# One Strassen level in the first product of the second MoE, on 768-token tiles, with its weights kept in DRAM

## The chip, the cores and the metric

The kernel runs on one core of one Trainium2 chip. TensorE (PE in the rows) multiplies matrices, VectorE (DVE), ScalarE (ACT) and GpSimd (POOL) work element by element, SyncE (SP) issues most DMAs. The metric is the device time of one execution in microseconds, as a median of several executions; lower is better.

## What is computed

Attention with a local and a downsampled part gives 2304 tokens of width 512; two MoE-like blocks follow. The last one, on which the change works, is `moe2`:

```python
def _moe_ref(x, w1, w2, w3, w_out):
    h = np.maximum(np.maximum(x @ w1, x @ w2), x @ w3)
    return h @ w_out                      # d_ff = 768

def _moe2_ref(x, w_in, w_out):            # x: 2304 x 512, d_ff = 2048
    h = np.maximum(x @ w_in, 0.0)
    return (h * h @ w_out)
```

The weights arrive as float64 words (128x512 of them are 512 KB) and are decoded to fp32 on the chip.

## The kernel before

Every fp32 product is made of three float32r matmuls (`mm3`): each operand is split into a rounded part `hi` and a rest `lo`, and hi·hi, hi·lo and lo·hi are summed in PSUM. `hi` is a ScalarE or VectorE copy with rounding, `lo` a subtraction on VectorE or GpSimd.

The tokens of a batch element (576) stand in two halves of 256 and 320. The program goes through the four batch elements; while TensorE does the first MoE (`moe1`) of element b, the other engines prepare the attention of element b+1. A table of tokens (`CFG`) gives the order: `G01` is one gate unit (three 4x3-matmul products of half 0, feature block 1), `Y02` one output unit of `moe1`, whose result goes to DRAM (`yscr`). `CFG["last"]` is the stretch for the last element, with `e` for one decoded weight tile of `moe2`. TensorE's instructions stand in the order in which they are written; a scheduler places those of the other engines, except that VectorE's order was also written out by hand from this stretch on.

`moe2` works on six tiles t of 384 tokens (`T2`). For each of 16 blocks f of 128 features, `in_unit` makes x·w_in (12 matmuls of 384 columns, tile `i`) into one of four PSUM banks, ScalarE and VectorE make relu, square and the split (`r`, `g`, `gh`, `gl`), and `out_unit`, called one block later, adds the block's share to three output banks (9 matmuls of 512 columns, tile `po`). All 32 weight tiles stay in SBUF after the first tile; they are decoded (`split_late`) during `last` and t = 0: VectorE rebiases (L98), shifts (L135), joins (L107, L110) and rounds (L143), GpSimd subtracts (L144). Raw words land in three buffers (`stg`).

Of the kernel before, what the change touches and what calls it, by code (L numbers as in the profile page):

```python
# [8 lines left out]
F32 = mybir.dt.float32  # L9
F32R = mybir.dt.float32r  # L10
# [8 lines left out]
P = 128  # L19
# [17 lines left out]
    "t0": "1111110201211120",  # L37
# [16 lines left out]
        "e e e G13 e e G02 e G11 e G12 G00 G10 e e G03 e G01 G14 G15 e Y13 G04 e Y10 e G05 e e e "  # L54
        "Y12 Y03 Y02 Y00 Y11 Y01 e e"
# [5 lines left out]
def local_global_attention__then__moe_kernel(  # L61
# [18 lines left out]
    T2 = 384  # L80
# [7 lines left out]
        for b in range(B)  # L88
    ]
# [40 lines left out]
    def split_late(items):  # L130
        parts = []
        work = [raw_words(src, name) for src, name, *_ in items]
        for low, high in work:
            rebias(high)
            nc.vector.tensor_scalar(  # L135
                out=low, in0=low, scalar1=29, scalar2=None, op0=ALU.logical_shift_right
            )
            join(low, high, low)
        for (src, name, pool, tag, bufs), (low, high) in zip(items, work):
            w = low.bitcast(F32)  # L140
            hi = pool.tile([P, 512], F32R, tag=tag, name=f"hi_{name}", bufs=bufs)
            lo = pool.tile([P, 512], F32R, tag=tag, name=f"lo_{name}", bufs=bufs)
            nc.vector.tensor_copy(hi, w)  # L143
            nc.gpsimd.tensor_tensor(out=lo, in0=w, in1=hi.bitcast(F32), op=ALU.subtract)  # L144
            parts.append((hi, lo))
        return parts

    def mm3(ps, whi, wlo, xhi, xlo, first, last):
        nc.tensor.matmul(ps, whi, xhi, start=first, stop=False)  # L149
        nc.tensor.matmul(ps, whi, xlo, start=False, stop=False)  # L150
        nc.tensor.matmul(ps, wlo, xhi, start=False, stop=last)  # L151
# [322 lines left out]

    w2_t = {}
    w2_todo = [(kind, f) for f in range(NF2) for kind in ("i", "o")]

    def load_w2(n=1):
        keys = w2_todo[:n]
        at = 2 * NF2 - len(w2_todo)  # L480
        del w2_todo[:n]
        items = []
        for i, (kind, f) in enumerate(keys):
            where = (w2, "w2", 12) if at + i < 6 else (wpool, "w", 36) if at + i < 24 else (gp, "w2", 16)
            items.append(((wi2 if kind == "i" else wo2)[f], f"{kind}2{f}", *where))
        if items:
            w2_t.update(zip(keys, split_late(items)))

    yt = {}
    NT2 = NT // T2  # L490

    def load_y(t, gq, pool):
        hi = pool.tile([P, NP, T2], F32R, tag="yh", name=f"yh{t}", bufs=1)
        lo = pool.tile([P, NP, T2], F32R, tag="yl", name=f"yl{t}", bufs=1)
        for k0 in range(0, NP, 2):
            raw = gq.tile([P, 2, T2], F32, tag="yr", name=f"yr{t}{k0}", bufs=1)
            t0, done = t * T2, 0
# [14 lines left out]
        yt[t] = (hi, lo)

    with tc.manual_schedule(engines={ENG.PE}):
# [26 lines left out]
        dve_order = ExitStack()  # L541
        dve_order.enter_context(tc.manual_schedule(engines={ENG.DVE}))
        at.close()
        w2 = ctx.enter_context(tc.tile_pool(name="w2", bufs=12, reuse_waits="tile"))
        gq = ctx.enter_context(tc.tile_pool(name="gq", bufs=1, reuse_waits="tile"))
        ps_o = ctx.enter_context(tc.tile_pool(name="ps_o", bufs=1, space=PSUM, reuse_waits="tile"))
        load_y(0, gq, gq)
        run(B - 1, CFG["last"])
        p1.close()

        gp = ctx.enter_context(tc.tile_pool(name="gp", bufs=2, reuse_waits="tile", side="right"))
        ps_i = ctx.enter_context(tc.tile_pool(name="ps_i", bufs=4, space=PSUM, reuse_waits="tile", side="right"))
        g_t = {}
        po = {}

        def in_unit(t, f):
            ps = ps_i.tile([P, 512], F32, tag="i", name=f"i{t}_{f}")
            hi, lo = w2_t["i", f]
            yhi, ylo = yt[t]
            for kc in range(NP):  # L560
                ks = slice(kc * P, (kc + 1) * P)
                mm3(ps[:, 0:T2], hi[:, ks], lo[:, ks], yhi[:, kc, :], ylo[:, kc, :], kc == 0, kc == NP - 1)
            r = gp.tile([P, T2], F32, tag="r", name=f"r{t}_{f}")
            g = gp.tile([P, T2], F32, tag="g", name=f"g2{t}_{f}")
# [11 lines left out]
        def out_unit(t, f):
            if f == 0:
                po[t] = [
                    ps_o.tile([P, DM], F32, tag=f"o{i}", name=f"po{t}_{i}") for i in range(T2 // P)
                ]  # L580
            ghi, glo = g_t.pop((t, f))
            whi, wlo = w2_t["o", f]
            for i in range(T2 // P):
                ts = slice(i * P, (i + 1) * P)
                mm3(po[t][i], ghi[:, ts], glo[:, ts], whi, wlo, f == 0, f == NF2 - 1)
                if f == NF2 - 1:
                    o = gp.tile([P, DM], F32, tag="ob", name=f"ob{t}_{i}", bufs=3)
                    if i % 2:
                        nc.vector.tensor_copy(o, po[t][i])
                    else:  # L590
                        nc.scalar.activation(out=o, in_=po[t][i], func=AF.Copy)
                    r0 = t * T2 + i * P
                    nc.sync.dma_start(out=out[r0 : r0 + P, :], in_=o)
# [62 lines left out]
```

## Time and profile before

| | |
|---|---|
| median of three executions | 874.84 us (874.76 to 878.05) |
| the profiled execution | 878.28 us, its span 876.4 us |
| TensorE busy | 833.2 us, 95% of the span |
| VectorE, ScalarE, GpSimd busy | 477.7, 278.6, 214.0 us |
| mean granted TensorE clock | 0.985 |
| `moe2`, from its first matmul to the last output copy | 462.9 to 872.0 us |

The span runs from the first to the last instruction of the profiled execution. Busy shares are an average over very different stretches, so the stretches below are read one by one.

### The profile page before, as it was taken

Reading aid. Unit: us, or ns where it says so; the run is one execution under the profiler, and the core shown is the slowest. Engines: PE = TensorE matmul, PEld = TensorE weight load, DVE = VectorE, ACT = ScalarE, POOL = GpSimd, SP = SyncE. Lnnn points to the kernel's source line nnn. Section 1 sums busy time; section 2 is a strip of 40 time slices with the busy share of each in tenths; the row PEclk is TensorE's granted clock in tenths of the full one; section 3 lists DMA queues with packets and bytes.
Section 4 is the critical chain, followed back from the end, with each engine's and each line's share of the span. In section 5 each row is a group of like instructions: output and inputs, shape, how many; then the busy total and the mean of one; then the engine's idle time right before and its main releaser. Section 6 shows DMA issues by size and latency. Waiting matters only on the chain.

```text
span 876.4 us, 15330 instructions
## 1 busy us (share of the span) xinstructions
PE 833.2 (95%) x6160; PEld 770.2 (88%) x6160; DVE 477.7 (55%) x938; ACT 278.6 (32%) x669; POOL 214.0 (24%) x260
## 2 busy tenths in 40 slices
PE   5588989999999999998998999999999999999997
PEld 4377989999999999998997889989999899989996
DVE  7998996525663375676789984223223223223222
ACT  3455533413342233421113333223223223223222
POOL 4745484400533032142135333001001001000000
PEclk9997999999999999998999999999999999999999
DMA  7735443400232011143245332002002001000001
GB/s 242 222 109 174 132 148 93 141 16 29 80 98 75 1 56 59 32 142 106 73 139 167 123 120 73 1 0 73 1 1 73 1 1 54 1 1 37 1 1 37
DMA packets 39831, 64.15 MB, mean 73 GB/s; under 512 B 4464, under 2 KB 23760, under 8 KB 39760
## 3 DMA queue, kind: packets, MB, share of 16 engines
q1 hardware_dynamic: 35152, 58.46, 21.5%
q10 hardware_dynamic: 4608, 4.72, 1.6%
q8 instruction: 48, 0.79, 0.4%
q14 instruction: 23, 0.19, 0.1%
HBM read 53.73 MB, written 9.44 MB: 72 GB/s over the span
## 4 chain that ended last, share of the span: by engine, by line
PE 83%; DVE 10%; DMA 3%; issue 1%; ACT 1%; POOL 0%; SPq 0%; DVEq 0%; ACTq 0%; POOLq 0%
PE g L149 8%; PE g L150 8%; PE g L151 7%; PE po L151 7%; PE po L150 7%; PE po L149 7%; PE i L149 7%; PE i L151 7%; PE i L150 7%; PE yp L149 3%; PE yp L151 3%; PE yp L150 3%; DMA q<-in_qT 1%; DMA raw_g<-in_wg 1%; DVE lo_g L126 1%
## 5 line engine op out<-in xcount | busy, mean ns | idle before, releaser
L149 PE MATMUL g<-xhi,hi_g 128*128 128x256 f32 (+1 forms) x576 | 177.0, 307 | 6.6 <-DVE c L407 6.6
L150 PE MATMUL g<-xlo,hi_g 128*128 128x256 f32 (+1 forms) x576 | 173.9, 302 | 1.5 <-DVE xlo L368 1.5
L151 PE MATMUL g<-xhi,lo_g 128*128 128x256 f32 (+1 forms) x576 | 174.0, 302 | 0.0
L567 DVE TENSOR_TENSOR g<-r 128x384 f32<-128x384 f32 x80 | 46.1, 577 | 193.3 <-ACT r L565 193.3
L149 PE MATMUL i<-yh,hi_i 128*128 128x384 f32 x384 | 129.6, 338 | 0.5 <-ACT ys L433 0.5
L151 PE MATMUL i<-yh,lo_i 128*128 128x384 f32 x384 | 129.4, 337 | 0.0
L150 PE MATMUL i<-yl,hi_i 128*128 128x384 f32 x384 | 129.3, 337 | 0.0
L149 PEld LDWEIGHTS g<-xhi,hi_g 128*128 128x128 f32 x576 | 112.4, 195 | 9.0 <-DVE c L407 7.6
L565 ACT ACTIVATE r<-i 128x384 f32<-128x384 f32 x96 | 47.2, 491 | 227.1 <-PE i L151 227.1
L151 PE MATMUL po<-hi_o,gl 128*128 128x512 f32 x288 | 114.3, 397 | 2.0 <-DVE gl L573 2.0
L149 PE MATMUL po<-hi_o,gh 128*128 128x512 f32 x288 | 113.8, 395 | 1.6 <-ACT gh L572 1.6
L150 PEld LDWEIGHTS g<-xlo,hi_g 128*128 128x128 f32 x576 | 113.0, 196 | 1.7 <-DVE xlo L368 1.7
L150 PE MATMUL po<-lo_o,gh 128*128 128x512 f32 x288 | 114.1, 396 | 0.0
L151 PEld LDWEIGHTS g<-xhi,lo_g 128*128 128x128 f32 x576 | 112.1, 195 | 0.0
L573 DVE TENSOR_TENSOR gl<-g,gh 128x384 fp32r<-128x384 f32 x96 | 54.5, 568 | 54.1 <-ACT gh L572 54.1
L407 DVE TENSOR_TENSOR c<-g,c 128x256 f32<-128x256 f32 (+1 forms) x96 | 43.6, 455 | 69.2 <-PE g L151 67.4
L149 PEld LDWEIGHTS i<-yh,hi_i 128*128 128x128 f32 x384 | 72.1, 188 | 4.9 <-ACT ys L433 0.7
L150 PEld LDWEIGHTS i<-yl,hi_i 128*128 128x128 f32 x384 | 72.1, 188 | 4.1
L509 POOL TENSOR_TENSOR yl<-yr,yh 128x384 fp32r<-128x384 f32 x24 | 26.8, 1135 | 196.7 <-ACT yh L508 196.7
L151 PEld LDWEIGHTS i<-yh,lo_i 128*128 128x128 f32 x384 | 72.1, 188 | 0.0
L151 PEld LDWEIGHTS po<-hi_o,gl 128*128 128x128 f32 x288 | 54.2, 188 | 17.7 <-DVE gl L573 4.6
L572 ACT ACTIVATE gh<-g 128x384 fp32r<-128x384 f32 x96 | 50.3, 524 | 49.0 <-DVE g L567 46.5
(1057 smaller groups left out, 1380.0 us busy)
## 6 DMA issues: line engine op xcount, KB each, us to landing
raw_o<-in_wo SPq DMA_DIRECT2D x22, 512.0 KB
raw_g<-in_wg SPq DMA_DIRECT2D x18, 512.0 KB
raw_i<-in_wi SPq DMA_DIRECT2D x16, 512.0 KB
k<-in_kT SPq DMA_DIRECT2D x16, 291.0 KB
q<-in_qT SPq DMA_DIRECT2D x16, 288.0 KB
v<-in_vP SPq DMA_DIRECT2D x32, 144.0 KB
out_y<-ob SPq DMA_DIRECT2D x18, 256.0 KB
vw<-in_vP SPq DMA_DIRECT2D x16, 175.0 KB
```

What stands on the lines that cost most here:

```text
L126: eng.tensor_tensor(out=lo, in0=w, in1=hi.bitcast(F32), op=ALU.subtract)
L149: nc.tensor.matmul(ps, whi, xhi, start=first, stop=False)
L150: nc.tensor.matmul(ps, whi, xlo, start=False, stop=False)
L151: nc.tensor.matmul(ps, wlo, xhi, start=False, stop=last)
L407: nc.vector.tensor_tensor(out=c, in0=ps[:, 0:N], in1=c, op=ALU.max)
L509: nc.gpsimd.tensor_tensor(out=lo[:, kc], in0=raw[:, kc - k0], in1=hi[:, kc].bitcast(F32), op=ALU.subtract)
L565: nc.scalar.activation(out=r, in_=ps[:, 0:T2], func=AF.Relu)
L567: nc.vector.tensor_tensor(out=g, in0=r, in1=r, op=ALU.mult)
L572: nc.scalar.activation(out=ghi, in_=g, func=AF.Copy)
L573: nc.vector.tensor_tensor(out=glo, in0=g, in1=ghi.bitcast(F32), op=ALU.subtract)
```

## The change

`moe2` now takes three tiles of 768 tokens, and eight quads q of 256 features each. One quad's product x·w_in is a 2x2 block product (384 tokens x 256 inputs by 256 inputs x 128 features, twice each way), and is made with seven block products P1 to P7 in place of eight, by Winograd's form of Strassen's method. A block product is 6 matmuls of 384 columns, into two PSUM banks in turn (`x`, `y`); P2 is added onto P1's bank and P3 onto P5's after VectorE or ScalarE have read them. Sums of token blocks (`S1` to `S4`, `y_sums`) and of weight blocks (`sums` in `decode_quad`) are made by VectorE, and so are the sums of products: `u2`, `u3` and three of the four output blocks `c`, each read from PSUM with a second input from SBUF. The output matmuls of a quad (12 groups of 3) are spread between the products of the next quad.

A quad's six pairs of weight tiles (`i0` to `i3`, `o0`, `o1`, hi and lo) live in four sets of buffers for eight quads. So each decoded quad is also stored to a DRAM scratch (`wscr`, 12 stores), and tiles 1 and 2 read four of the eight quads back (`load_quad`). Quads 0 to 2 are decoded during `last`, quads 3 to 7 during tile 0. `last` has lost its `e` tokens, and its units stand in the order of the features. VectorE's order is left to the scheduler.

```diff
-    T2 = 384
+    T2 = 768
+    TH = T2 // 2
+    NT2 = NT // T2
+    NQ = NF2 // 2
+    PRODUCTS = (
+        ("P1", "A11", "i0", 0), ("P6", "S2", "i1", 256), ("P2", "A12", "i0", 256), ("P7", "S3", "i2", 0),
+        ("P5", "S1", "i1", 0), ("P4", "A22", "i2", 256), ("P3", "S4", "i3", 0),
+    )
...
+    def split_cut(q, c, w, c0=0):
+        n = w.shape[-1]
+        hi, lo = w2_t[q][c + "h"][:, c0 : c0 + n], w2_t[q][c + "l"][:, c0 : c0 + n]
+        nc.scalar.activation(out=hi, in_=w, func=AF.Copy)
+        nc.gpsimd.tensor_tensor(out=lo, in0=w, in1=hi.bitcast(F32), op=ALU.subtract)
...
+        def sums():
...
+            nc.vector.tensor_tensor(out=t1, in0=b12, in1=b11, op=ALU.subtract)
+            nc.vector.tensor_tensor(out=t3, in0=b22, in1=b12, op=ALU.subtract)
+            nc.vector.tensor_tensor(out=t2, in0=b22, in1=t1, op=ALU.subtract)
+            nc.vector.tensor_tensor(out=t4, in0=t2, in1=b21, op=ALU.subtract)
...
+        return [
+            lambda: begin("f0", wi2[f]),
+            lambda: begin("f1", wi2[f + 1]),
+            both,
+            other,
+            sums,
+            lambda: (split_cut(q, "i1", tb["f0"]), begin("o0", wo2[f]), stores("i0", "i3")),
+            lambda: (split_cut(q, "i2", tb["f1"]), begin("o1", wo2[f + 1]), stores("i1", "i2")),
+            lambda: last("o0", "o0"),
+            lambda: (last("o1", "o1"), stores("o0", "o1")),
+        ]
...
+                if p == "P1":
+                    got["p1"] = f("p1", "p", 1)
+                    A.activation(out=got["p1"], in_=d, func=AF.Copy)
+                elif p == "P6":
+                    got["u2"] = f("u2", "u2", 1)
+                    V.tensor_tensor(out=got["u2"], in0=d, in1=got["p1"], op=ALU.add)
...
+                elif p == "P7":
+                    got["u3"] = f("u3", "u3", 1)
+                    V.tensor_tensor(out=got["u3"], in0=d, in1=got["u2"], op=ALU.add)
+                elif p == "P5":
+                    e = f("c", "c22", 3)
+                    V.tensor_tensor(out=e, in0=d, in1=got["u3"], op=ALU.add)
+                    square("22", e)
...
+                for call in outs[len(outs) * j // 7 : len(outs) * (j + 1) // 7]:
+                    call()
...
+        spread(0, 0, [lambda a=a: y_split(0, a, nc.vector) for a in ("S1", "A22", "S4")], 0)
+        spread(0, 0, decode_quad(3))
+        for q in range(4, NQ):
+            spread(0, q - 3, decode_quad(q), 2)
+        turns = [list(range(NQ)), [4, 5, 6, 7, 0, 1, 2, 3], list(range(NQ))]
```

Where the instructions went is seen in the built programs. VectorE before, one block of t = 0 (`raw_o210` is a raw weight tile, `gl0_4` the rest of the squared features of block 4 that `out_unit` multiplies):

```order
L98 TENSOR_SCALAR raw_o210_6107<-raw_o210_6107 128x512
L135 TENSOR_SCALAR raw_o210_6107<-raw_o210_6107 128x512
L107 SCALAR_TENSOR_TENSOR raw_o210_6107<-raw_o210_6107 128x512
L110 SCALAR_TENSOR_TENSOR raw_o210_6107<-raw_o210_6107 128x512
L143 CAST hi_o210_6113<-raw_o210_6107 128x512
L573 TENSOR_TENSOR gl0_4_6144<-g20_4_6140,gh0_4_6143 128x384
```

VectorE now, half of quad 3 of tile 0 (`u303` is u3 of tile 0, quad 3; L108 rebiases, L117 and L120 join, of raw words of quads 5 and 6):

```order
L737 TENSOR_TENSOR u303_6660<-P7_03_6653,u203_6608 128x384
L671 TENSOR_TENSOR gl0311_6636<-c1103_6632,gh0311_6635 128x384
L740 TENSOR_TENSOR c2203_6684<-P5_03_6677,u303_6660 128x384
L714 SCALAR_TENSOR_TENSOR c2203_6684<-c2203_6684 128x384
L108 TENSOR_SCALAR raw_o1_5_6618<-raw_o1_5_6618 128x512
L671 TENSOR_TENSOR gl0322_6688<-c2203_6684,gh0322_6687 128x384
L744 TENSOR_TENSOR c2103_6720<-u303_6660,P4_03_6713 128x384
L117 SCALAR_TENSOR_TENSOR raw_o1_5_6618<-raw_o1_5_6618 128x512
L714 SCALAR_TENSOR_TENSOR c2103_6720<-c2103_6720 128x384
L120 SCALAR_TENSOR_TENSOR raw_o1_5_6618<-raw_o1_5_6618 128x512
L748 TENSOR_TENSOR c1203_6743<-P5_03_6677,u203_6608 128x384
L671 TENSOR_TENSOR gl0321_6724<-c2103_6720,gh0321_6723 128x384
```

Decoding and the reads of PSUM for which TensorE waits now alternate on one in-order engine. SyncE's queue before, in the same stretch, held raw loads alone:

```order
L93 DMA raw_i211_6147<-in_wi2 128x512
L93 DMA raw_o211_6187<-in_wo2 128x512
L93 DMA raw_i212_6257<-in_wi2 128x512
L93 DMA raw_o212_6267<-in_wo2 128x512
L93 DMA raw_i213_6353<-in_wi2 128x512
```

SyncE's queue now, as quad 4 is stored and quad 5 begun (`s4i1l` is the scratch copy of the lo part of cut i1 of quad 4):

```order
L501 DMA s4i1h_121<-w4i1h_6337 128x512
L501 DMA s4i1l_122<-w4i1l_6338 128x512
L103 DMA raw_o1_4_6437<-in_wo2 128x512
L501 DMA s4i2h_123<-w4i2h_6339 128x512
L501 DMA s4i2l_124<-w4i2l_6340 128x512
L103 DMA raw_f0_5_6468<-in_wi2 128x512
L501 DMA s4o0h_127<-w4o0h_6343 128x512
L501 DMA s4o0l_128<-w4o0l_6344 128x512
L103 DMA raw_f1_5_6492<-in_wi2 128x512
```

Each raw load now stands behind stores that wait for ScalarE and GpSimd.

## Rows read from the trace of the kernel before

**Rows 1.** The page's busy times: us (share of span) x instructions.

```profile
PE 833.2 (95%) x6160; PEld 770.2 (88%) x6160; DVE 477.7 (55%) x938; ACT 278.6 (32%) x669; POOL 214.0 (24%) x260
```

**Rows 2.** Stretches: length, then PE, PEld, DVE, ACT, POOL busy, clock, DMA share, GB/s.

```profile
0.00:378.90 378.90, 347.89 (x3570) 327.44 (x3571) 253.76 (x566) 142.81 (x393) 141.30 (x205) 0.98 0.33 100
378.90:462.90 84.00, 79.99 (x577) 79.32 (x575) 65.27 (x114) 15.49 (x37) 26.41 (x20) 0.96 0.38 120
462.90:535.00 72.10, 68.46 (x338) 60.08 (x339) 63.92 (x94) 27.06 (x54) 31.38 (x22) 1.00 0.38 115
602.00:872.00 270.00, 269.91 (x1346) 242.93 (x1344) 75.91 (x133) 73.85 (x148) 10.60 (x11) 1.00 0.06 20
```

**Rows 3.** PE in order of time, steady `moe2`: start, duration, instruction.

```profile
600.56 0.34 PE L149 MATMUL i<-yh,hi_i 128*128 128x384 f32 x1
...
602.67 0.40 PE L149 MATMUL po<-hi_o,gh 128*128 128x512 f32 x1
...
604.76 0.34 PE L149 MATMUL i<-yh,hi_i 128*128 128x384 f32 x1
```

**Rows 4.** PE's waits from 380 us on: total us, times, longest.

```profile
PE g L149 <- DVE c L407: 3.5, 2, 2.8
PE po L151 <- DVE gl L573: 2.0, 4, 1.1
PE po L149 <- ACT gh L572: 1.6, 1, 1.6
```

**Rows 5.** PE in order of time around the longest of these waits.

```profile
397.54 0.63 PE L149 MATMUL g<-xhi,hi_g 128*128 128x320 f32 x1 [2.77 <-DVE c L407]
397.97 0.47 PE L150 MATMUL g<-xlo,hi_g 128*128 128x320 f32 x1
...
403.55 0.31 PE L150 MATMUL g<-xlo,hi_g 128*128 128x320 f32 x1
403.70 0.31 PE L151 MATMUL g<-xhi,lo_g 128*128 128x320 f32 x1
```

**Rows 6.** VectorE's groups in 462.9 to 535 us: busy us, mean ns, idle before.

```profile
L573 DVE TENSOR_TENSOR gl<-g,gh 128x384 fp32r<-128x384 f32 x16 | 9.6, 599 | 6.4 <-ACT gh L572 6.4
L98 DVE TENSOR_SCALAR raw_o<-raw_o 128x512 f32<-128x512 f32 x8 | 9.0, 1123 | 0.0
L107 DVE SCALAR_TENSOR_TENSOR raw_o<-raw_o 128x512 uint32<-128x512 uint32 x8 | 6.3, 782 | 0.3
```

**Rows 7.** The split `gl` in 535 to 800 us, the same columns.

```profile
L573 DVE TENSOR_TENSOR gl<-g,gh 128x384 fp32r<-128x384 f32 x63 | 35.5, 563 | 37.6 <-ACT gh L572 37.6
```

**Rows 8.** VectorE reading PSUM in 378.9 to 462.9 us, two widths.

```profile
L407 DVE TENSOR_TENSOR c<-g,c 128x320 f32<-128x320 f32 x12 | 5.9, 489 | 4.9 <-PE g L151 4.5
L407 DVE TENSOR_TENSOR c<-g,c 128x256 f32<-128x256 f32 x12 | 5.1, 423 | 4.0 <-PE g L151 3.4
```

**Rows 9.** GpSimd's subtraction in 395 to 560 us.

```profile
L144 POOL TENSOR_TENSOR lo_o<-raw_o,hi_o 128x512 fp32r<-128x512 f32 x14 | 20.5, 1465 | 47.6 <-DVE hi_o L143 39.5 <-PE g L151 5.5 <-issue 2.7
```

**Rows 10.** VectorE in order of time around 501 us.

```profile
500.34 0.70 DVE L110 SCALAR_TENSOR_TENSOR raw_i<-raw_i 128x512 uint32<-128x512 uint32 x1
...
501.42 0.42 DVE L98 TENSOR_SCALAR raw_o<-raw_o 128x512 f32<-128x512 f32 x1
501.75 1.54 DVE L135 TENSOR_SCALAR raw_o<-raw_o 128x512 uint32<-128x512 uint32 x1
```

**Rows 11.** GpSimd at the same time.

```profile
501.58 1.43 POOL L144 TENSOR_TENSOR lo_i<-raw_i,hi_i 128x512 fp32r<-128x512 f32 x1 [3.63 <-DVE hi_i L143]
```

**Rows 12.** SyncE's DMA queue: packets, MB, share of 16 engines' span.

```profile
q1 hardware_dynamic: 35152, 58.46, 21.5%
```

**Rows 13.** Issue of half a token tile (0.79 MB in two DMAs) on SyncE.

```profile
385.61 0.89 SPq L503 DMA_DIRECT2D yr<-y  x2
```

**Rows 14.** ScalarE: the first use of that half, and the last output copy.

```profile
389.40 0.94 ACT L508 ACTIVATE yh<-yr 128x384 fp32r<-128x384 f32 x2 [0.58 <-DMA yr<-y]
...
871.95 0.60 ACT L591 ACTIVATE ob<-po 128x512 f32<-128x512 f32 x1 [0.79 <-PE po L151]
```

More of the change, by code (lines that the diff above doesn't have):

```diff
@@ L88, in local_global_attention__then__moe_kernel @@
         for b in range(B)
+    ]
+    wscr = [
+        {
+            c + e: yd.tile([P, 256 if c == "i3" else 512], F32, name=f"s{q}{c}{e}", tag=f"s{q}{c}{e}")
+            for c in CUT
+            for e in "hl"
+        }
+        for q in range(NQ)
     ]
@@ L128, in split_mid, with mm3 @@
         return parts
[L130 to L151, printed above, removed]
+    def mm3(ps, whi, wlo, xhi, xlo, first, last, more=False):
+        nc.tensor.matmul(ps, whi, xhi, start=first, stop=False, skip_group_check=more)
+        nc.tensor.matmul(ps, whi, xlo, start=False, stop=False, skip_group_check=more)
+        nc.tensor.matmul(ps, wlo, xhi, start=False, stop=last, skip_group_check=more)
     p1 = ExitStack()
@@ new lines, in load_quad, with part, y_sums, load @@
+    def load_quad(q):
+        def part(cuts, new=False):
+            if new:
+                quad_tiles(q)
+            for c in cuts:
+                n = 256 if c == "i3" else 512
+                for e in "hl":
+                    nc.sync.dma_start(out=w2_t[q][c + e][:, 0:n].bitcast(F32), in_=wscr[q][c + e])
+        return [lambda: part(CUT[:4], True), lambda: part(CUT[4:])]
+    def y_sums(t):
+        blocks = y2_t[t] = {}
+        def load():
+            raw = yq.tile([P, NP, T2], F32, tag="yr", name=f"yr{t}")
@@ L576, in out_unit @@
[L576 to L593, printed above, removed]
@@ L595, in local_global_attention__then__moe_kernel @@
[L595 to L608 removed]
+        yq = ctx.enter_context(tc.tile_pool(name="yq", bufs=1, reuse_waits="tile"))
@@ new lines, in local_global_attention__then__moe_kernel @@
+        ps_i = ctx.enter_context(tc.tile_pool(name="ps_i", bufs=1, space=PSUM, reuse_waits="tile"))
+        back = y_sums(0)
+        back += [lambda a=a: y_split(0, a, nc.vector) for a in EARLY]
+        for q in range(3):
+            back += decode_quad(q)
+        units = CFG["last"].split()
+        done = 0
+        for i, token in enumerate(units):
+            run(B - 1, token)
+            while done < len(back) * (i + 1) // len(units):
+                back[done]()
+                done += 1
@@ new lines, in local_global_attention__then__moe_kernel, with product @@
+        p1.close()
+        gp = ctx.enter_context(tc.tile_pool(name="gp", bufs=1, reuse_waits="tile", side="right"))
+        ps_o = ctx.enter_context(tc.tile_pool(name="ps_o", bufs=1, space=PSUM, reuse_waits="tile"))
+        po = {}
+        def product(t, q, ps, a, c, c0, first):
+            whi, wlo = w2_t[q][c + "h"], w2_t[q][c + "l"]
+            yhi, ylo = y2_t[t][a + "x"]
+            for kc in range(2):
+                ks = slice(c0 + kc * P, c0 + (kc + 1) * P)
+                mm3(ps[:, 0:TH], whi[:, ks], wlo[:, ks], yhi[:, kc, :], ylo[:, kc, :], first and kc == 0, kc == 1, not first)
@@ new lines, in local_global_attention__then__moe_kernel @@
+        for t, k in ((1, 0), (1, 1), (1, 2), (1, 3), (2, 0), (2, 1), (2, 2), (2, 3)):
+            one, two = load_quad(turns[t][k + 4])
+            spread(t, k + 1, [one], 1)
+            spread(t, k + 2, [two], 1)
+        for t in range(NT2 - 1):
+            spread(t, 5, y_sums(t + 1), 0, 2)
+            for j, (_, a, _, _) in enumerate(PRODUCTS):
+                spread(t, NQ - 1, [lambda t=t, a=a, j=j: y_split(t + 1, a, nc.gpsimd if j % 2 else nc.vector)], j)
+        outs = []
+        y_split(0, "S3", nc.vector)
@@ L611 @@
+        for t in range(NT2):
+            for k, q in enumerate(turns[t]):
+                outs = quad(t, k, q, outs, between[t, k])
+        for call in outs:
+            call()
 def kernel(**inputs):
```

218 lines of the change are left out of this document (146 added, 72 removed).

## The prediction

> **What bounds the kernel now.** I read the page's busy times first: TensorE is busy 95% of the span, VectorE 55%, GpSimd 24% [rows 1]. Such a share says nothing of a single stretch, so the windows by stage come next [rows 2]. From 602 us on, TensorE is busy 269.91 of 270 us while VectorE has 76 us of work: there only fewer or shorter matmuls save time. From 378.9 to 535 us the picture is another. In the last stretch of the first MoE and in the first tile of `moe2`, VectorE is busy 65.27 of 84.00 and 63.92 of 72.10 us, and GpSimd adds 26 and 31 us. That is where the weights are decoded, and the change puts more work for both engines there.
>
> TensorE's own timeline gives the price of a matmul: 12 of 384 columns take 602.67 − 600.56 = 2.11 us, 0.176 each, and 9 of 512 columns 2.09 us, 0.232 each [rows 3]. Its waits from 380 us on are few: 3.5 us on VectorE's `c` at the gates, 3.6 us on the splits `gl` and `gh` at the start of `moe2` [rows 4]. After the longest, 2.77 us, the next 22 matmuls stand (403.55 − 397.54) / 22 = 0.273 us apart, against 0.15 from 403.55 on: the level of 1.2 GHz, where 22 x 0.123 = 2.7 us are lost [rows 5].
>
> **What is removed.** Before, `moe2` has 96 blocks of 12 matmuls, 1152; now 24 quads of 7 x 6, 1008. 144 matmuls at 0.176: −25.3 us. The output matmuls stay 864. A quad takes TensorE 42 x 0.176 + 36 x 0.232 = 15.74 us. The two waits at the gates with the slow clock behind one of them come from VectorE's handwritten order, in which decoding stood before `c`; the scheduler's order has the `c` first: −3.5 − 2.7 = −6.2, with 1.0 given back because seven passes over 128x768 tokens (0.95 us each, from the slope of 423 to 489 ns for 64 more columns [rows 8]) now stand among the first gates. Four PSUM banks hide most of these. The 3.6 us of waits at the start of `moe2` go with the code in which they stood.
>
> **The first quad** has no output groups to put between its products, which follow each other at 1.06 us, 7.4 in all. Before TensorE can take a bank for quad 1, VectorE must do four token splits of 768 (3.8 us), four reads of PSUM at 0.56 (the same slope, at 384 columns), and the three passes between them (1.8), and the first split can start some 2 us late, behind ScalarE's last copy of the first MoE: 9.8 us. +2.4.
>
> **Quads 1 to 5 of the first tile** are the heart of it. From u2 of quad 1 to u2 of quad 6, VectorE's order holds 17 rebias, 34 joins, 16 weight sums of 256 columns, 4 token sums of 768 and 65 passes of 384 over products. At the durations of the first tile before, 1.1 us for a rebias, 0.78 for a join, 0.6 for a pass in SBUF [rows 6], 0.56 for the 25 that read PSUM, 0.42 for a sum (as the 256-column row [rows 8]), that is 18.7 + 26.5 + 6.7 + 3.8 + 24 + 14 = 93.7 us. TensorE needs 5 x 15.74 = 78.7. VectorE is in order, and u2, u3 and `c` are what TensorE waits for before it may write a bank again; a bank is free some 3.5 us late before that hurts, once, not per quad. So +15. The lower bound is the same list undisturbed: 0.42 for a rebias, 0.70 for a join [rows 10], 0.56 for a pass [rows 7]: 78 us, +0. The disturbance is seen in one place: a tensor_scalar of 0.42 us took 1.54 when it came 0.17 us after a GpSimd subtraction of 1.43 had begun [rows 10, 11]. The upper bound is that the two engines take turns throughout, below under the rivals. I take the durations as they stood in the first tile before, since GpSimd's share was the same 43% there.
>
> The Trainium skill (SBUF — State Buffer, Who interferes with whom) says that GpSimd and VectorE share one pair of ports as an exclusive lock, and that VectorE operations with two SBUF inputs take part in it, not only the fast single-input ones. The 1.54 us agrees for the latter; for the two-input `gl` the rows show 599 ns beside a busy GpSimd against 563 without, and no pure case. By that rule the term would be +17 to +31 in place of +15.
>
> **Raw words.** A decoded quad loads 4 x 524 KB and stores 2.88 MB, 4.98 MB. The SyncE queue moved 58.46 MB in 21.5% of 876.4 us, 310 GB/s when all is busy [rows 12]; so 16.1 us a quad, under the 18.7 that VectorE needs: hidden, with little to spare. Half a token tile took 3.8 us from issue to use [rows 13, 14], so a raw tile some 3. Between the last weight sum and the next quad's first rebias stand about 13 VectorE instructions, 8 us, which must cover ScalarE's and GpSimd's split, the issue and the landing, 6.5 to 7.5 us. I take +1, between 0 and the rival below.
>
> **Small terms.** The tokens of tile 2 are asked for when GpSimd has split the last block of tile 1, and take about 6.3 us to land (3.8 and 0.79 MB more at 310 GB/s), while VectorE waits for them in quad 0 of tile 1 with u3 behind: +1, between 0 and 3. One wait long enough to lower the clock: +1, between 0 and 5 (2.7 each). The last output copy finds two buffers in place of three and waits for the DMA of the copy two before it: +0.9, between 0 and 1.9 (from the 4.45 us between 871.95 and the span's end [rows 14], less the 2.8 us between the two). The reloads of tiles 1 and 2 have over 40 us before their first use, VectorE needs 13 x 0.56 = 7.3 of 15.74 us there, and GpSimd nothing but token splits: no cost.
>
> **Sum.** −25.3 − 6.2 + 1.0 − 3.6 + 2.4 + 15 + 1 + 1 + 1 + 0.9 = −12.8 us on a span of 876.4 us: 863.6. The profiled execution took 878.28 us, 1.9 outside its span, and is 3.4 above the median; taken off the median of 874.84, the sum gives 862.0.
>
> **The rivals.**
> - Decoding stays covered. For it: the undisturbed list needs 78 us, no more than TensorE. Against it: the rows of the first tile, where VectorE was never undisturbed. Without the 15 and the clock: 846.
> - VectorE and GpSimd take turns. Its place is the same five quads. All but the 25 reads of PSUM shut GpSimd out: 78 − 14 = 64 us undisturbed, and GpSimd has the like of 22 subtractions at 1.465 us [rows 9], 32: 96 us if the PSUM reads all run beside GpSimd, 110 if none does, +17 to +31. The first tile before speaks for it: 63.92 + 31.38 is 95 us in 72.1, and the excess of 23 is about what the VectorE rows are longer than undisturbed. This is the skill's rule above. At +24: 871.
> - Raw words come late, the side on which the change loses. Place: each rebias at VectorE's head waits for a DMA that stands behind stores on SyncE; u2, u3 and `c` wait behind it. Each 256 KB store ahead of a raw tile adds 0.85 us. Four ahead of each quad's first load cost 3.4 us a quad; if the 17 waits add up to 13 us the gain is gone, and from 17 us (1 us each) the kernel is slower by over 0.5%. With 5 us a quad and more at the other loads: 880 to 890.
> - The saving is not had in the steady quads: a bank is not read in time in every quad. For it: two banks in place of four. Against it: each read has 3 us, VectorE and ScalarE are half idle. At 1 us a quad: 885.
>
> **How the numbers follow.** Forecast (853 to 870) 0.42, covered 0.20, taking turns beyond it 0.14, late raw words 0.15, steady quads late 0.06, slow clock over much of the first tile 0.03 (870). The range runs from the covered case to the point where late words have taken all: 846 to 878. Half a per cent, 4.4 us, is about what a measurement of this kernel can tell from no change. Faster by more: the first two, half of the third and a little of the others, 0.70. Within: 0.15. Slower: 0.15.
>
> **What would show it.** PE matmuls on the products 1008 at 0.176 and quads of 15.7 us in tiles 1 and 2; the first tile 140 to 146 us long in place of 126, its waits on VectorE's u2, u3 and `c` reads and not on ScalarE; VectorE over 95% busy there with rebias near 1.1 us; the gates' wait of 2.77 gone. VectorE idle behind raw DMAs in quads 1 to 5 would show the third rival, joins at 1 us and more the second. I am wrong if the first tile takes under 132 or over 155 us, or a quad of tile 1 over 16.5.

## The result, and the profile after

The changed kernel takes 866.02 us in the median of four executions (864.85 to 866.37), the kernel before 874.80: a ratio of 0.989, with a 95% interval of 0.9864 to 0.9916. The forecast was 862.0, so that 8.8 of the 12.8 us were gained. The two profiled executions stand further apart than the medians: that of the kernel before took 878.28 us, 3.5 above its median, that of the changed kernel 864.85, 1.2 below. Its span is 863.1 us, against a forecast of 863.6.

Between these two executions the total agrees to half a microsecond, in part by this luck; in which stage the 4.6 us lie that they have over the medians, no trace shows. The stages do not agree, and they are what the experiments had to explain. The page's busy times of the changed kernel, to be read beside [rows 1]:

```profile
PE 809.9 (94%) x6016; PEld 741.7 (86%) x6016; DVE 561.0 (65%) x1072; ACT 298.5 (35%) x679; POOL 220.7 (26%) x258
```

TensorE has 144 instructions fewer, VectorE 134 more and 83 us more to do. The stretches, with the columns of [rows 2], are cut here at the last attention product of the last batch element (372.25, where the last stretch of the first MoE begins), the first product of `moe2` (462.52), u2 of quads 1 and 6 of the first tile (477.41, 570.49), u2 of the second tile's first quad (600.48) and the end of the matmuls:

```profile
0.00:372.25 372.25, 336.95 (x3438) 315.95 (x3439) 254.38 (x565) 141.34 (x384) 139.32 (x204) 0.94 0.32 100
372.25:462.52 90.27, 89.32 (x714) 88.14 (x710) 60.46 (x99) 36.85 (x77) 23.39 (x18) 1.00 0.61 203
462.52:477.41 14.89, 12.52 (x65) 10.78 (x64) 12.81 (x17) 9.83 (x18) 7.84 (x5) 1.00 0.54 185
477.41:570.49 93.08, 82.79 (x395) 70.18 (x394) 85.67 (x138) 39.38 (x72) 38.34 (x25) 1.00 0.69 238
570.49:600.48 29.99, 29.99 (x151) 26.93 (x150) 18.80 (x32) 11.65 (x19) 5.88 (x3) 1.00 0.09 30
600.48:859.00 258.52, 258.05 (x1269) 229.72 (x1267) 128.89 (x225) 58.87 (x110) 5.92 (x3) 1.00 0.33 110
```

The same cuts in the trace of the kernel before lie at 367.22 (that attention product) and 462.88 (the first product). The two profiled executions then differ so:

| stage | before | after | forecast | measured |
|---|---|---|---|---|
| up to the last attention product | 367.22 | 372.25 | 0 | +5.0 |
| last stretch of the first MoE | 95.66 | 90.27 | −5.2 | −5.4 |
| first product to last output copy | 409.07 | 396.87 | −8.5 | −12.2 |
| last output copy to the end | 4.45 | 3.71 | +0.9 | −0.7 |
| span | 876.4 | 863.1 | −12.8 | −13.3 |

The last row of that count, with [rows 14] for the kernel before, is ScalarE's last output copy:

```profile
859.39 0.60 ACT L687 ACTIVATE ob<-po 128x512 f32<-128x512 f32 x1 [2.14 <-PE po L143]
```

A loss of 5.0 us that the forecast did not have lies before any instruction of `moe2` on TensorE, and it is hidden in the total by 3.7 us in `moe2` and 1.6 at the end that came out better. It is no accident of one execution: in the eight traces of this document that decode quad 0 so early, this attention product stands at 370.8 to 373.3 us, in the kernel before at 367.2 and in its variant below (before_lovec) at 366.7.

The stretch that the forecast called the heart, u2 of quad 1 to u2 of quad 6, takes 93.08 us where the forecast had 93.7 and TensorE needs 78.7. TensorE's waits from 462.52 to 600.48 us, in total, how often, and the longest:

```profile
PE P L141 <- DVE u L737: 4.6, 3, 1.9
PE P L141 <- DVE c L748: 3.5, 4, 1.2
PE P L141 <- DVE c L744: 1.3, 1, 1.3
PE P L141 <- DVE c L740: 1.2, 2, 1.0
PE P L141 <- ACT c L732: 1.0, 2, 0.7
PE P L141 <- ACT p L726: 0.7, 1, 0.7
PE P L141 <- DVE u L729: 0.2, 1, 0.2
```

10.8 of 12.5 us are waits for VectorE's reads of a bank (u2, u3, `c`), none is over 2 us, and the granted clock stays at 1.00. VectorE's largest groups in that stretch, with the columns of [rows 6]:

```profile
L671 DVE TENSOR_TENSOR gl<-c,gh 128x384 fp32r<-128x384 f32 x21 | 16.8, 800 | 2.4 <-ACT gh L670 2.2
L714 DVE SCALAR_TENSOR_TENSOR c<-c 128x384 f32<-128x384 f32 x15 | 10.4, 695 | 0.1
L117 DVE SCALAR_TENSOR_TENSOR raw_o<-raw_o 128x512 uint32<-128x512 uint32 x9 | 9.0, 996 | 0.2
L733 DVE TENSOR_TENSOR c<-c 128x384 f32<-128x384 f32 x5 | 4.4, 885 | 0.0
L108 DVE TENSOR_SCALAR raw_o<-raw_o 128x512 f32<-128x512 f32 x9 | 3.8, 422 | 2.6 <-DMA raw_o<-in_wo 2.6
L729 DVE TENSOR_TENSOR u<-P,p 128x384 f32<-128x384 f32 x6 | 3.3, 549 | 0.0
```

The forecast wanted VectorE over 95% busy and the rebias at 1.1 us. It is 92% busy (85.67 of 93.08), the rebias of `raw_o` takes 0.42 and that of `raw_f` 0.52, and the long ones are the passes with two inputs in SBUF: `gl` 0.80, the first join 1.00. The reads of PSUM (u2) stay at 0.55. GpSimd in order of time, and VectorE beside it, show why:

```profile
507.23 1.41 POOL L496 TENSOR_TENSOR w4o1l<-raw_o,w4o1h 128x512 fp32r<-128x512 f32 x1 [2.65 <-ACT w4o1h L495]
510.02 1.60 POOL L496 TENSOR_TENSOR w5i0l<-raw_f,w5i0h 128x512 fp32r<-128x512 f32 x1 [1.38 <-ACT w5i0h L495]
```

VectorE at the same time:

```profile
507.38 0.54 DVE L744 TENSOR_TENSOR c<-u,P 128x384 f32<-128x384 f32 x1
507.85 1.33 DVE L120 SCALAR_TENSOR_TENSOR raw_f<-raw_f 128x512 uint32<-128x512 uint32 x1
509.11 0.54 DVE L671 TENSOR_TENSOR gl<-c,gh 128x384 fp32r<-128x384 f32 x1
509.57 0.55 DVE L714 SCALAR_TENSOR_TENSOR c<-c 128x384 f32<-128x384 f32 x1
510.04 0.41 DVE L108 TENSOR_SCALAR raw_f<-raw_f 128x512 f32<-128x512 f32 x1
510.38 0.54 DVE L748 TENSOR_TENSOR c<-P,u 128x384 f32<-128x384 f32 x1
510.85 1.32 DVE L117 SCALAR_TENSOR_TENSOR raw_f<-raw_f 128x512 uint32<-128x512 uint32 x1
```

Each of the two GpSimd subtractions has several VectorE passes beside it. The one that reads PSUM takes its 0.54, the rebias at 510.04 its 0.41. The join after them, 0.68 when alone, ends some 0.5 us after the subtraction does (509.18 against 508.64, 512.17 against 511.62), as if it had begun its work only then. This is the forecast's rival "VectorE and GpSimd take turns", and it became the first theory to test.

To put a size on it: the sum of all VectorE durations in the stretch less each form's count times its shortest duration there is the excess. For `gl` it is 21 x (0.80 − 0.55) = 5.3 us; over all forms it is 19.1 us, beside 38.3 us of GpSimd.

The 5.0 us before the last stretch start at one row of TensorE. It is the last of five transpositions for the second batch element:

```profile
139.66 0.30 PE L298 MATMUL t10B<-const,sm10B 128*70 128x128 f32 x1 [3.81 <-DVE x3210F L352]
```

In the trace before, all five stood together, without a wait:

```profile
136.13 0.74 PE L306 MATMUL t10B<-const,sm10B 128*70 128x128 f32 x5
```

VectorE does x3210F at 139.18 us, behind three rebias, six joins and four sums of quad 0's raw words that it began at 127.63. Before, one raw tile's decoding stood there. The scheduler had pulled the decoding of a weight that is needed at 462 us forward to 127. Behind the wait the granted clock is 0.50, the level of 1.2 GHz, for a while (142 to 144 us), and from the first of the five to the product behind them (o10B) it takes 15.25 us (135.21 to 150.46) in place of 9.52 (136.13 to 145.65): 5.7 more. The granted clock was also lower than before in the first part of this execution (0.50 in place of 1.00 from 20 to 40 us), but at the first transposition TensorE was still 0.9 us ahead of the trace before, so the 5.0 us are not from there.

### The profile page after: what moved, and what is told of

It reads as the page before. It is cut to its first block, busy times and chain, and to the rows that moved or that the text cites. A ratio compares the mean times of both kernels' runs of the same rounds, so it can differ in the third digit from the quotient of the medians.

```text
span 863.1 us, 15554 instructions
## 1 busy us (share of the span) xinstructions
PE 809.9 (94%) x6016; PEld 741.7 (86%) x6016; DVE 561.0 (65%) x1072; ACT 298.5 (35%) x679; POOL 220.7 (26%) x258
## 5 line engine op out<-in xcount | busy, mean ns | idle before, releaser
L670 ACT ACTIVATE gh<-c 128x384 fp32r<-128x384 f32 x96 | 50.3, 524 | 149.6 <-DVE c L714 133.0
L671 DVE TENSOR_TENSOR gl<-c,gh 128x384 fp32r<-128x384 f32 x96 | 62.2, 649 | 39.7 <-ACT gh L670 39.4
L141 PE MATMUL yp<-hh,hi_o 128*128 128x256 f32 (+1 forms) x192 | 58.8, 306 | 0.0
L143 PE MATMUL yp<-hh,lo_o 128*128 128x256 f32 (+1 forms) x192 | 57.5, 299 | 0.0
L142 PE MATMUL yp<-hl,hi_o 128*128 128x256 f32 (+1 forms) x192 | 57.5, 299 | 0.0
L714 DVE SCALAR_TENSOR_TENSOR c<-c 128x384 f32<-128x384 f32 x72 | 43.4, 604 | 1.9
L141 PEld LDWEIGHTS yp<-hh,hi_o 128*128 128x128 f32 x192 | 37.0, 193 | 0.8 <-issue 0.6
L143 PEld LDWEIGHTS yp<-hh,lo_o 128*128 128x128 f32 x192 | 37.1, 193 | 0.0
L142 PEld LDWEIGHTS yp<-hl,hi_o 128*128 128x128 f32 x192 | 37.1, 193 | 0.0
L217 POOL TENSOR_TENSOR v<-v 72x256 f32<-72x256 f32 x32 | 26.0, 829 | 38.8 <-DMA v<-in_vP 38.8
```

The lines of the kernel that those rows point to most:

```text
L141: nc.tensor.matmul(ps, whi, xhi, start=first, stop=False, skip_group_check=more)
L142: nc.tensor.matmul(ps, whi, xlo, start=False, stop=False, skip_group_check=more)
L143: nc.tensor.matmul(ps, wlo, xhi, start=False, stop=last, skip_group_check=more)
L217: nc.gpsimd.tensor_tensor(out=v4[:, 0:2], in0=v4[:, 0:2], in1=v4[:, 2:4], op=ALU.add)
L670: nc.scalar.activation(out=ghi, in_=c, func=AF.Copy)
L671: nc.vector.tensor_tensor(out=glo, in0=c, in1=ghi.bitcast(F32), op=ALU.subtract)
```

## The experiments

Ratios are to the kernel before on the same chip. "The stretch" is that from u2 of quad 1 to u2 of quad 6 of the first tile, 93.08 us in the changed kernel.

**GpSimd's subtractions, taken away.** First theory: VectorE and GpSimd shut each other out.

```diff
-        nc.gpsimd.tensor_tensor(out=lo, in0=w, in1=hi.bitcast(F32), op=ALU.subtract)
+        nc.scalar.activation(out=lo, in_=w, func=AF.Copy)
```

> GpSimd's subtractions of the weight splits are replaced by a second rounded copy on ScalarE, so the lo parts of the weights are not the rests; nothing else changes. The stretch is that from u2 of quad 1 to u2 of quad 6 of the first tile, 93.1 us in the changed kernel, where TensorE's instructions need 78.7. Theory A, VectorE and GpSimd shut each other out: the passes with two SBUF inputs fall to their shortest durations (join 0.69, gl 0.55), about 19 us of the sum of durations go, VectorE's busy time falls from 85.7 to about 68, and the stretch to 79 to 83: the kernel at 853 to 857. Theory B, the passes are long by themselves or by SBUF traffic of the DMAs: the stretch stays above 90 and the time within 2 us of 866. Theory C, raw words set the pace: VectorE waits for DMAs instead, stretch 86 to 93.

853.96 us, ratio 0.9749 (0.9721 to 0.9778). The stretch takes 78.95 us and TensorE is busy in all of it:

```profile
477.88:556.83 78.95, 78.95 (x392) 70.80 (x391) 65.80 (x134) 49.52 (x93) 0.00 (x0) 1.00 0.76 264
```

VectorE's same groups there:

```profile
L671 DVE TENSOR_TENSOR gl<-c,gh 128x384 fp32r<-128x384 f32 x21 | 11.6, 552 | 0.9 <-ACT gh L670 0.7
L117 DVE SCALAR_TENSOR_TENSOR raw_o<-raw_o 128x512 uint32<-128x512 uint32 x8 | 5.5, 685 | 0.3 <-ACT raw_o L114 0.3
L108 DVE TENSOR_SCALAR raw_o<-raw_o 128x512 f32<-128x512 f32 x8 | 3.4, 423 | 3.4 <-DMA raw_o<-in_wo 3.4
L733 DVE TENSOR_TENSOR c<-c 128x384 f32<-128x384 f32 x5 | 2.8, 558 | 3.1 <-ACT c L732 2.9
L729 DVE TENSOR_TENSOR u<-P,p 128x384 f32<-128x384 f32 x6 | 3.3, 556 | 3.3 <-PE P L143 3.2
```

`gl` fell from 0.80 to 0.55, the join from 1.00 to 0.69, `c` from 0.89 to 0.56; the rebias is 0.42 now for `raw_f` too, and the reads of PSUM are as they were. DMAs moved more per second than before (264 against 238 GB/s), so DMA traffic does not lengthen the passes, and theory B falls. The stretch gave back 14.1 us and the median 12.1: from the first product to u2 of quad 1, where ScalarE now has the extra copies, it takes 18.8 us in place of 14.9.

**The same subtractions on VectorE.**

```diff
-        nc.gpsimd.tensor_tensor(out=lo, in0=w, in1=hi.bitcast(F32), op=ALU.subtract)
+        nc.vector.tensor_tensor(out=lo, in0=w, in1=hi.bitcast(F32), op=ALU.subtract)
```

> The same subtractions on VectorE, so that GpSimd has no part in decoding and VectorE 25 more passes of 128x512 in the stretch of 93.1 us, at 0.6 us from start to start, 15 in all. Theory A (the two engines shut each other out): the excess of about 19 us goes as the 15 come, and the stretch is 88 to 93; the kernel within 4 us of 866. Theory B (the passes are long whoever else works): 15 to 17 us come on top, stretch 108, kernel about 880.

852.14 us, ratio 0.9725 (0.9699 to 0.9751): better than theory A had it, with the stretch at 82.81 in place of 88 to 93.

```profile
473.99:556.80 82.81, 81.30 (x399) 71.87 (x398) 75.19 (x151) 37.71 (x68) 0.00 (x0) 1.00 0.67 238
```

VectorE does 13 instructions more than in the changed kernel's stretch and is busy 10.5 us less. Of the subtractions 20 fall into it, where the expectation counted 25, and seven other passes of the decoding no longer do, which is a part of the 10.5 us. Moving work onto the engine that set the pace made it faster, since each subtraction takes 0.68 us there and cost VectorE 0.76 in the mean while GpSimd did it (19.1 us for 25).

**And made twice on GpSimd**, for quads 3 to 7.

> Each subtraction of quads 3 to 7 is made twice on GpSimd, the second time with the same result: 25 more in the stretch of 93.1 us, 33 to 38 us. Theory A (a VectorE pass with two SBUF inputs waits while GpSimd has the port): the excess of 19.1 us over the shortest durations grows to 30 to 38, the reads of PSUM stay at 0.55, the stretch is 106 to 114 and the kernel at 879 to 887. Rival (GpSimd lengthens VectorE only where it happens to start together with it, and has room): stretch 93 to 97.

884.24 us, ratio 1.01 (1.0076 to 1.0124), the stretch 106.69 us:

```profile
482.65:589.34 106.69, 86.02 (x391) 72.08 (x390) 101.77 (x132) 37.10 (x67) 61.76 (x44) 0.97 0.52 180
```

Its groups keep the pattern, `gl` 0.93 and the reads of PSUM 0.55:

```profile
L673 DVE TENSOR_TENSOR gl<-c,gh 128x384 fp32r<-128x384 f32 x21 | 19.5, 931 | 1.8 <-ACT gh L672 1.7
L731 DVE TENSOR_TENSOR u<-P,p 128x384 f32<-128x384 f32 x5 | 2.7, 548 | 0.0
```

The excess is 35.5 us for 61.8 us of GpSimd. So from none to one to two subtractions the excess is under 1, 19.1 and 35.5 us: 0.50 and 0.57 us on VectorE for each microsecond that GpSimd works. In the first tile of the kernel before it was 17.4 for 31.4 [rows 2], 0.55.

The Trainium skill (SBUF — State Buffer, Who interferes with whom) has a VectorE instruction with two SBUF inputs contend with a GpSimd instruction that reads SBUF, and one with at most one SBUF input stay clear of it unless it runs in a two-port mode. The runs agree on the first, for `gl`, squares and joins grew, and on the second for the reads of PSUM, which never did. The rebias, with its one input in SBUF, grew at times (to 0.70 in the mean for `raw_f` in double_lo); in which mode it runs, no run here shows.

**VectorE's list made shorter, GpSimd left.** relu and square go to ScalarE.

```diff
-                V.scalar_tensor_tensor(out=c, in0=c, scalar=0.0, in1=c, op0=ALU.max, op1=ALU.mult)
+                A.activation(out=c, in_=c, func=AF.Relu)
+                A.activation(out=c, in_=c, func=AF.Square)
...
-                    V.tensor_tensor(out=e, in0=e, in1=e, op=ALU.mult)
+                    A.activation(out=e, in_=e, func=AF.Square)
```

> relu and square of all four blocks of a quad on ScalarE in place of VectorE: 20 passes, 14.8 us of VectorE's durations, leave the stretch of 93.1 us, and 35 go to ScalarE (17 us on 39 of 93). Theory A (VectorE's list sets the stretch, and TensorE has 78.7 to do): it falls to 79 to 84, the kernel to 854 to 858. Rival: the DMAs of raw words and stores set the pace, and VectorE waits for them: stretch over 88, kernel 862 or more. In tiles 1 and 2 a quad stays at 15.8.

861.39 us, ratio 0.9832 (0.9801 to 0.9863); the stretch 90.24. The expectation of 79 to 84 was wrong. VectorE lost 9.7 us of busy time, but the stretch lost only 2.8. (Another 3.0 us were gained ahead of it: from the first product to u2 of quad 1 it takes 11.93 us in place of 14.89.) The excess is still 17.4 us, beside 35.7 of GpSimd. VectorE's waits there:

```profile
DVE raw_o L108 <- DMA raw_o<-in_wo: 6.2, 4, 2.8
DVE gl L671 <- ACT gh L670: 4.8, 5, 1.4
DVE raw_f L108 <- DMA raw_f<-in_wi: 1.3, 2, 1.0
```

Raw words (7.5 us, 4.4 before) and ScalarE's longer chain to `gh` (4.8, 2.2 before) took the place of the passes. Two further runs ask whether the scratch traffic makes the words late; they store the hi parts alone.

```diff
-        for e in "hl":
+        for e in "h":
             nc.sync.dma_start(out=wscr[q][c + e], in_=w2_t[q][c + e][:, 0:n].bitcast(F32))
...
-                    nc.sync.dma_start(out=w2_t[q][c + e][:, 0:n].bitcast(F32), in_=wscr[q][c + e])
+                    nc.sync.dma_start(out=w2_t[q][c + e][:, 0:n].bitcast(F32), in_=wscr[q][c + "h"])
```

> Only the hi parts of a quad are stored to the DRAM scratch (6 stores for 12), and the reload reads them for hi and lo, so the lo parts of reloaded weights are copies of hi; the time of everything else stays. In the stretch of 93.1 us some 7 of 22 MB of DMA traffic go, and each raw load has half the stores ahead of it. Theory A (the two engines shutting each other out sets the stretch; raw words cost VectorE's 4.4 us of waits at most): stretch 88 to 94, kernel 861 to 867. Rival (stores ahead of raw loads set it): stretch 80 to 86, kernel under 859.

866.43 us, ratio 0.9897 (0.9871 to 0.9922), no different from the changed kernel. The stretch fell to 89.71, VectorE's waits for raw words from 4.4 to 1.6; the last stretch of the first MoE grew by 2.3 us, so that nothing is left in the total. That is theory A with its 4 us of raw words.

> square_scalar with half of the scratch stores (the lo parts of reloaded weights are copies of hi). With the squares on ScalarE alone the stretch from u2 of quad 1 to u2 of quad 6 was 90.2 us with VectorE busy 76.0 and 7.5 us of waits for raw words. Theory C (behind VectorE's list stood the raw words, which took the place of the work removed): stretch 82 to 86, VectorE's waits for raw words under 3 us. Theory A alone (GpSimd's subtractions, which stay): stretch 87 to 91.

861.52 us, ratio 0.9838 (0.9815 to 0.9861), the stretch 87.92. That lies in theory A's range, but with half of the stores VectorE still waits 8.9 us for raw words, so theory C's cure does not touch its cause. SyncE's own queue shows a reason that traffic does not touch. Its waits from 480 to 500 us:

```profile
SPq L501 <- ACT w3o1h L495: 7.9, 1, 7.9
SPq L501 <- ACT w4i3h L495: 7.0, 1, 7.0
SPq L103 <- POOL w3o1l L496: 1.8, 1, 1.8
```

and the issues behind the first and the third:

```profile
486.67 0.33 SPq L501 DMA_DIRECT2D s3o1h<-w3o1h  x1
488.85 0.33 SPq L103 DMA_DIRECT2D raw_o<-in_wo  x1
```

The raw load stands behind a store that waits 7.9 us for ScalarE's split, and then for its buffer until GpSimd has read it. Lateness comes in part from the order in the queue, as the forecast's third rival had it.

**Quad 0's decoding made to start late**, by a one-column copy from a token tile of the last element into its raw buffer ahead of the load.

```diff
+        if after is not None:
+            nc.scalar.activation(out=raw.bitcast(F32)[:, 0:1], in_=after, func=AF.Copy)
         nc.sync.dma_start(out=raw, in_=src)
...
+            after = x_t[B - 1, 0][0][:, 0, 0:1].bitcast(F32) if q == 0 else None
-            low, high = raw[key] = raw_words(src, f"{key}_{q}")
+            low, high = raw[key] = raw_words(src, f"{key}_{q}", after)
```

> The first raw loads of quad 0 wait for a token tile of the last batch element (a one-column ScalarE copy into the buffer), so that its decoding leaves the place at 127 to 139 us, ahead of x3210F, to which the scheduler had moved it. Theory A (ten VectorE instructions there made TensorE wait 3.8 us for the transposed scores, and the time was never given back): the start of the last stretch goes from 372.2 back to about 367.5, the kernel to 860.5 to 862. Rival (the 5 us come from the slower clock in the first 60 us of that execution): the start stays at 371 or more, the kernel at 865 to 867. In the stretch of the first tile nothing changes: 93 us.

862.44 us, ratio 0.984 (0.9813 to 0.9868). The last attention product comes at 365.92 us, 6.3 earlier than in the changed kernel, and the wait is gone from its transpositions:

```profile
131.99 0.74 PE L300 MATMUL t10B<-const,sm10B 128*70 128x128 f32 x5
...
347.91 0.74 PE L300 MATMUL t31B<-const,sm31B 128*70 128x128 f32 x5 [2.18 <-DVE pt32F L282]
...
365.92 0.65 PE L325 MATMUL o33F<-pt33F,vw 70*64 70x64 f32 x16
```

The stretch of the first tile stays at 93.2 us. That the decoding's place cost the 5.7 us there is shown: from the first of the five transpositions to o10B it takes 9.52 us again (131.99 to 141.51). The rest of the 6.3 us is a balance. TensorE came to the transpositions 3.2 us earlier, 1.7 of them by the element's first transposition (112.42 against 114.13), before which no decoding had moved and this execution had a higher granted clock (0.95 against 0.81). And 2.6 us were lost again at 343 to 348 us, where quad 0 is now decoded (337 to 349) and TensorE has a new wait of 2.18 us for VectorE: the new place is better, not free. The whole is also 1.3 us better than the kernel before, which had some decoding at the first place too.

**An eighth product**, P3 added a second time in every quad.

> P3 is made twice, its second copy added onto the same bank, so that every quad has 8 block products of 6 matmuls again; the output is that of a wrong sum. If each product is worth its 1.06 us of matmuls wherever TensorE is the bound, and the quads 1 to 5 of the first tile are set by VectorE, those five hide theirs: 16 quads of tiles 1 and 2 give 16.9 us, the others of tile 0 3.2, 20 in all, 884 to 888; a quad of tiles 1 and 2 goes from 15.85 to 16.9, and the stretch from u2 of quad 1 to u2 of quad 6 stays at 93 to 95. Rival (TensorE is the bound in the first tile too): the stretch grows by 5.3 and the kernel is at 891. Rival (the chain of banks is the bound in tiles 1 and 2): a quad there stays under 16.4.

889.0 us, ratio 1.0157 (1.0124 to 1.019). By spans it is 22.0 us over the changed kernel, by medians 23.0, a little above the 20 expected. u2 of the second tile's first quad and of the last quad, 15 quads apart, stand at

```profile
606.76 0.56 DVE L731 TENSOR_TENSOR u<-P,p 128x384 f32<-128x384 f32 x1 [1.82 <-PE P L143]
...
859.21 0.56 DVE L731 TENSOR_TENSOR u<-P,p 128x384 f32<-128x384 f32 x1 [1.92 <-PE P L143]
```

16.83 us a quad against 15.85, so 0.98 of the 1.06 us of a product's matmuls are had there. In the stretch 2.5 of 5.3 us are seen: the slack behind VectorE hides about half. The 144 matmuls that the change removed are worth 22 to 23 of the forecast 25.3 us.

**The two gains together:** the subtractions on VectorE and the late quad 0.

> The lo parts of the weights on VectorE and the late first load of quad 0 together. If the two work in different places, their gains add: 13.9 and 3.6 us off 866.0, 848.5; 846 to 851. If delaying quad 0's decoding puts it where VectorE with its new subtractions is full, the gain of the second is lost: 852.

846.51 us, ratio 0.967 (0.9647 to 0.9693): the best of all, 2.3% under the changed kernel and 3.3% under the one before. The gains add, with 2.0 us more than the 848.5 expected. Its stretch takes 81.82 us, with 5.3 us of VectorE's waits for raw words, and two runs tried to take these away by issuing the stores from GpSimd's queue.

```diff
-            nc.sync.dma_start(out=wscr[q][c + e], in_=w2_t[q][c + e][:, 0:n].bitcast(F32))
+            nc.gpsimd.dma_start(out=wscr[q][c + e], in_=w2_t[q][c + e][:, 0:n].bitcast(F32))
```

> lovec_late with the stores to the scratch issued from GpSimd's queue, which is idle there, so that no raw load stands behind a store that still waits for its data. Theory C (order in SyncE's queue makes the raw words late): VectorE's 5.3 us of waits for raw words in its stretch of 81.8 us go to under 2, the stretch to 79 or 80, the kernel from 846.5 to 843 to 845. Rival (the DMA engines' share, 0.68, makes them late, whatever the queue): no change, 846 to 847; worse, 848 and more, if the issues on GpSimd shut VectorE out.

858.14 us, ratio 0.9805 (0.978 to 0.9831), 11.6 us worse than without. The stretch did fall, to 79.95, with 2.4 us of waits for raw words, nearly as theory C has it; but from the first product to u2 of quad 1 it takes 23.1 us in place of 13.8. VectorE waited 6.6 us there for the token tile after this one, whose sums the scheduler now had ahead of u2 of quad 1. GpSimd is busy 22.9 us of the stretch with issuing the stores, and VectorE's excess there is 1.0 us: this kind of work on GpSimd did not lengthen its passes, the subtractions did. The second run makes that load wait for u3 of quad 4.

> lovec_late_queue, with the load of the next token tile made to wait for u3 of quad 4 (a one-column ScalarE copy into each part of its buffer), so that its four sums leave the place ahead of u2 of quad 1, where VectorE waited 6.6 us for that load and TensorE behind it for gl. Theory (the loss of lovec_late_queue is that wait and nothing of the queue itself): from the first product of moe2 to u2 of quad 1 it is 13 to 15 us again, in place of 23.1, the stretch to u2 of quad 6 stays at 78.7 to 81, and the kernel at 843 to 847. Rival (issues on GpSimd's queue slow VectorE or the loads by themselves): 18 us and more there, 850 or more.

857.73 us, ratio 0.9792 (0.9761 to 0.9823). The theory falls: the start of `moe2` still takes 19.3 us, and the wait for the tokens, now 7.6 us, has moved into the stretch, now 89.8 us. What is seen in the start is ScalarE, in order, at the first raw word:

```profile
470.50 0.69 ACT L116 ACTIVATE raw_o<-raw_o 128x512 uint32<-128x512 uint32 x1 [7.38 <-DMA raw_o<-in_wo]
```

Its load was issued at 463.53 and so took 7 us, beside ten stores issued from 460.39 to 465.93 that no longer wait in the same queue. That the stores' traffic delays it is not shown: in lovec_late the same load took 5.7 us (465.36 to 471.06), and ScalarE, which came to it later there, waited 1.3. No run changed the queue and left ScalarE's order as it was.

**The kernel before with its late subtractions on VectorE:** the same edit in the code that the change replaced.

> The kernel before, with the 32 subtractions of the late decoding on VectorE in place of GpSimd. Theory A: the excess in its first tile of moe2 (17.4 us of durations beside 31 us of GpSimd) goes, some 10 us of subtractions come; VectorE's busy time there falls, and part of TensorE's 7 us of waits at the gates and at the start of moe2 with it: 869 to 874. Rival: the waits come from the order in which VectorE's list is written, whatever its durations: 874 to 877.

880.95 us, ratio 1.0057 (1.0036 to 1.0078): slower. Its excess fell from 17.4 to 2.9 us, yet TensorE's wait for `c` at a gate grew from 2.8 us [rows 4] to 4.5. Both expectations were missed. That the handwritten order of VectorE decides who waits there, the rival's reason, fits the longer wait but is not shown: the two traces are only 1.5 us apart (877.9 and 876.4), and where the rest of the 5 us lies they do not tell. The lesson of lo_vector was seen only where the length of VectorE's list is the bound.

## Why the forecast was right in total and not in its parts

Right in total holds for the two profiled executions. By the medians a third of the forecast gain is missing, and in which stage stays open. The parts below are those of the two traces.

- **The matmuls removed, −25.3.** Right in kind, and some 10% large by the eighth product; most of what is missing lies in the stretch, where VectorE is the bound. Quads of tiles 1 and 2 take 237.78 / 15 = 15.85 us, forecast 15.74.
- **The gates, −6.2 + 1.0.** Right: the last stretch gives 5.4, its waits at the gates are 0.9 us and its clock 1.00.
- **What failed outright: that the change begins in the last stretch.** "Quads 0 to 2 are decoded during `last`" was read from the code, and the order of the part before it was not looked at. The scheduler's list had quad 0 at 127 us: +5.0.
- **The heart, +15.** 93.08 − 78.7 = +14.4, of which quads 6 and 7 gave back 1.5. The size is right and its making is not. The forecast added 17 rebias at 1.1 us and other rows of the first tile before, to 93.7 us of a VectorE that never stops. In truth 85.7 us are busy and 7.4 idle. Laid end to end the durations give 94.8 us, some 9 too much, since each pass starts some 0.08 us before the one ahead of it ends (above, `gl` ends at 509.11 + 0.54 = 509.65, and the square behind it starts at 509.57). Undisturbed, in lo_scalar, the list (134 of the 138 instructions) takes 65.8 us, not 78. The excess is 19.1 in place of 16, and lies on other instructions. The overlap of the passes and the idle time were both left out, and the two errors nearly cancelled: that 93.1 met 93.7 is luck.
- **The rivals.** "Covered" (846) is what the same quads do as soon as GpSimd is silent: 78.95 us. "Taking turns" is the mechanism of the 15 and not a case beyond it: a microsecond of GpSimd cost VectorE half of one, not the whole. The excess of 23 us that the forecast saw in the first tile before is 17.4 by the shortest durations. "Late raw words" was given +1; 4.4 us of VectorE's waits in the stretch are theirs, of which half_scratch gave back 3.4. "Banks late in every quad" fell: 0.1 us a quad.
- **Small terms.** The first quad cost about 4.0 us and not 2.4: from the first product to u2 of quad 1 it took 14.89, where seven products (7.4), one output group (0.7) and the 2.8 from P1 to u2 make 10.9. The passes of 1.2 to 1.7 us beside GpSimd are there too. In `moe2` the clock cost nothing. The tokens of tile 2 cost nothing: VectorE waited 3.4 us for them, TensorE 0.4 in all after 600 us. The tail cost nothing: the last output copy waited for TensorE, not for its buffer.
- **`moe2` as a whole, 3.7 better.** The heart gave 2.1 (12.9 in place of 15), the terms for raw words (whose waits lie in the heart already), tokens and clock gave 3; the first quad cost 1.6 and the steady quads 1.7 more than forecast. The rest, some 2 us, lies in the kernel before: its `moe2` took 5.9 us over its matmuls (409.07 less 96 x 4.20 [rows 3]), where the forecast counted 3.6.
- **The sign of 140 to 146 us for the first tile** was not met: 134.9 us lie between the first products of the first two tiles (462.52 and 597.37). The 126 beside it, 8 x 15.74, counts eight quads of output groups, and the last quad's 8.4 us (36 x 0.232) stand in the next tile.

## What to carry to other kernels

Where VectorE sets the pace, look at GpSimd's work in the same stretch before looking for VectorE work to move away: here a microsecond of subtractions on GpSimd put half a microsecond on VectorE's two-input passes, and taking the work back made the kernel 14 us faster. When a scheduler places new work, read its list from the start of the program, not from where the code stands: work with free inputs can be put in front of something urgent hundreds of microseconds early. And a total that agrees with the forecast proves little until its stages are laid side by side.

## What the hardware showed that was not expected

A VectorE pass held up by GpSimd shows no idle time: its row is longer. In one stretch the same join reads 0.68 us and 1.80 us, and VectorE looks 92% busy while its undisturbed work (85.7 us less the excess of 19.1) fills some 72%. Only the shortest duration of each form, or a run in which GpSimd is silent, tells the two apart.
